# A windowed-attention and gated-MLP kernel on one core: the listed order of its steps between 18 and 75 microseconds replaced by another

## The chip, the cores and the metric

The kernel runs on one core of one Trainium2 chip. A core has a matrix engine (TensorE, PE in the profile), a vector engine (VectorE, DVE), a scalar engine (ScalarE, ACT), GpSimd (POOL), SyncE (SP), which here issues nearly all loads and stores, and 16 DMA engines that carry them out. Each engine runs its own instructions strictly in the order in which they were given to it; engines wait for one another by semaphores. The metric is the device time of one execution in microseconds (us); lower is better.

## What is computed

Eight batch entries ("blocks" here) go through a causal attention with a window of 64 positions, and the result through a gated MLP in which one half is normalised, mixed over the positions and multiplied with the other half. Cut to what matters:

```python
# attention: q, k, v are (8, 8 heads, 576 positions, 64)
scores = scale * np.matmul(q, k.transpose(0, 1, 3, 2))
mask = (rel >= 0) & (rel < 64)
attn = softmax(np.where(mask, scores, -1e9))
x = (attn @ v).transpose(0, 2, 1, 3).reshape(8, 576, 512)
# gated MLP
h = np.maximum(x @ w_in, 0.0)                  # w_in (512, 1024)
u, v = h[..., :512], h[..., 512:]
v_n = (v - mean(v)) / np.sqrt(var(v) + 1e-6)
v_s = np.einsum('ts,bsd->btd', w_spatial, v_n) + b_spatial[None, :, None]
out = (u * v_s) @ w_out                        # float32
```

## The kernel before

The kernel is one long list of 1,111 named steps. A step is one small piece of work: one load, one cast, or one group of matmuls into one accumulator bank. The text `ORDER` at the top of the file gives for each step its engine and, where it needs a buffer, the number of that buffer, and `as_listed` hands the steps out in that order. Per engine the order in the text is the order of execution; between engines the order is kept only where data or a buffer passes on. So `ORDER` decides three things: in which order an engine works, which engine does a cast or copy that several can do, and which earlier work a step must wait for because it takes over its buffer. The order was made by a planner ahead of time; no planner runs in the kernel.

A name has a letter for the kind of step, then the block, then the part. For one block b:

- `ldk`, `ldq`, `ldv`: loads of k, q (576 KB, for one half of the heads) and v (five pieces of up to 128 KB); SP issues them (lines 401 and 422). `ck`, `cq`, `cv`: casts to float16; `tk`, `tq`: transposes on VectorE (line 408); `sl`, `su`, `s4`: copies that make a second v, shifted by 64 positions (lines 293 to 301, the helper `cp`).
- `S`: scores of 64 small matmuls into a pair of banks (line 470); `E`: exponential on ScalarE (477); `M`: masking on VectorE (480); `Z`: row sums on TensorE (493); `N`, `n`: logarithm and exponential on ScalarE, which give the inverse (519, 521); `P`: attention times v on TensorE (504); `X`: the product with the inverse on VectorE (512). The last 64 positions have their own steps with `_r`.
- `V`: the half of x @ w_in that is normalised (653; the fifth one at 666 also carries the last output rows of the block before it); `Vr`: relu on ScalarE (633); `Vb`, `Va`: statistics on VectorE (635, 637); `L1`, `L2`: their inverse square root on ScalarE; `A`: the normalisation on VectorE (692). `U`, `Ur`: the other half and its relu (708, 721). `G`, `Ge`: the mixing over positions and the product (738, 752). `O`, `Oe`, `st`: output matmul, copy and store (763, 610).
- Once, early: `ldwin`, `cwin` for the eight pieces of w_in (`cwin1..` belong to V, `cwin0..` to U; the last two digits are the input rows), `ldwsp`, `cwsp`, `W`, `We` for w_spatial, which is transposed on TensorE, `ldwo`, `cwo` for w_out, and 25 `D` steps of two matmuls each on zeros (791), which keep TensorE busy at the start.

Four single banks (0 to 3) and two pairs (0:1) are shared by all matmul steps. A step that takes a bank waits until the step that had it before was read: a V step's bank is free when its `Vr` has run, a G step's when its `Ge` has. The number behind a step's engine in `ORDER` is that bank or buffer. TensorE does attention for block b+1 between the matmuls of block b's MLP.

VectorE, ScalarE and GpSimd can all do the early casts and copies (blocks 0 and 1 and the weights); for later blocks ScalarE and GpSimd alone, since `cost(...)` leaves VectorE out. On GpSimd a cast of 1,152 columns is three instructions.

## Time and profile before

| | us |
|---|---|
| median of 3 runs | 201.6 (201.12 to 201.91) |
| the profiled execution, device time | 201.67 |
| its span on the core | 200.0 |
| TensorE busy, at a granted clock of 1.00 throughout | 189.5 |
| ScalarE busy | 166.7 |
| VectorE busy | 160.9 |
| GpSimd busy | 78.0 |

The span runs from the first to the last instruction of the core; 1.67 us of the device time lie around it. The page cuts the span in 40 slices of 5 us and shows the busy share of each in tenths:

```profile
PE   7788899999999999999999999999999999999992
...
DVE  4699959999998999799699899979957795647430
```

From the sixth slice on TensorE is 90% or more busy in every slice but the last. The same rows show how full VectorE is from 30 to 75 us. Busy times are shares of the engine's time, not of its speed.

### The profile page before, as it was taken

Reading aid. Unit: us, or ns where it says so; the run is one execution under the profiler, and the core shown is the slowest. Engines: PE = TensorE matmul, PEld = TensorE weight load, DVE = VectorE, ACT = ScalarE, POOL = GpSimd, SP = SyncE. Lnnn points to the kernel's source line nnn. Section 1 sums busy time; section 2 is a strip of 40 time slices with the busy share of each in tenths; the row PEclk is TensorE's granted clock in tenths of the full one; section 3 lists DMA queues with packets and bytes.
Section 4 is the critical chain, followed back from the end, with each engine's and each line's share of the span. In section 5 each row is a group of like instructions: output and inputs, shape, how many; then the busy total and the mean of one; then the engine's idle time right before and its main releaser. Section 6 shows DMA issues by size and latency. Waiting matters only on the chain.

```text
span 200.0 us, 7013 instructions
## 1 busy us (share of the span) xinstructions
PE 189.5 (95%) x2927; PEld 97.8 (49%) x2927; DVE 160.9 (80%) x306; ACT 166.7 (83%) x307; POOL 78.0 (39%) x147
## 2 busy tenths in 40 slices
PE   7788899999999999999999999999999999999992
PEld 2333435645446445654455545554465455444450
DVE  4699959999998999799699899979957795647430
ACT  2598789887999899997998999999999999467431
POOL 5232574784995397252745999000000000000000
PEclk9999999999999999999999999999999999999999
DMA  6997999999899866898959996996723003200345
GB/s 224 378 284 175 362 374 209 303 374 377 168 258 281 278 182 195 260 277 210 333 123 259 245 293 224 244 285 226 187 109 118 3 7 131 108 0 0 133 143 201
DMA packets 50276, 42.69 MB, mean 214 GB/s; under 512 B 39362, under 2 KB 39490, under 8 KB 50243
## 3 DMA queue, kind: packets, MB, share of 16 engines
q1 hardware_dynamic: 50018, 41.91, 70.5%
q8 instruction: 23, 0.38, 0.8%
q10 hardware_dynamic: 224, 0.33, 0.5%
q14 instruction: 11, 0.08, 0.2%
HBM read 32.79 MB, written 9.44 MB: 211 GB/s over the span
## 4 chain that ended last, share of the span: by engine, by line
PE 72%; ACT 9%; SPq 6%; DMA 5%; DVE 3%; issue 1%; POOL 1%
PE bank L738 18%; PE bank L763 13%; PE bank L653 12%; PE bank L708 10%; SPq L422 4%; PE pair L470 3%; PE bank L504 3%; PE bank L493 3%; PE bank L666 3%; DMA wi<-in_moe_w_in_dram 3%; PE bank L744 3%; DMA nk<-in_k_dram 2%; ACT vs L633 2%; ACT ru L721 2%; PE bank L713 2%; ACT e L477 1%
## 5 line engine op out<-in xcount | busy, mean ns | idle before, releaser
L738 PE MATMUL bank<-wspT,vn 128*128 128x512 f16 (+1 forms) x160 | 37.5, 379 | 0.0
L477 ACT ACTIVATE e<-pair 128x1024 f16<-128x1024 f32 x32 | 31.8, 1027 | 2.7 <-PE pair L470 2.4
L752 DVE TENSOR_TENSOR g<-bank,ru 128x512 f16<-128x512 f32 (+1 forms) x40 | 24.8, 631 | 10.9 <-PE bank L738 5.9
L653 PE MATMUL bank<-win,x 128*128 128x512 f16 x128 | 30.8, 379 | 1.0 <-POOL win L301 0.8
L708 PE MATMUL bank<-x,win 128*128 128x512 f16 x128 | 31.6, 379 | 0.0
L763 PE MATMUL bank<-wout,g 128*128 128x512 f16 x128 | 31.3, 379 | 0.0
L635 DVE BATCH_NORM_STATS2 st<-vs 128x6 f32<-128x512 f16 (+1 forms) x40 | 25.9, 670 | 3.8 <-ACT vs L633 3.5
L721 ACT ACTIVATE ru<-bank 128x512 f32<-128x512 f32 (+1 forms) x40 | 21.4, 562 | 8.4 <-PE bank L708 4.6
L633 ACT ACTIVATE vs<-bank 128x512 f16<-128x512 f32 (+1 forms) x40 | 22.9, 596 | 3.2 <-PE bank L653 2.3
L610 ACT COPY ob<-bank 128x512 f32<-128x512 f32 (+1 forms) x39 | 22.6, 589 | 3.3 <-PE bank L763 3.1
L512 DVE TENSOR_TENSOR x<-bank,lz 128x512 f16<-128x512 f32 x32 | 21.2, 683 | 4.9 <-PE bank L504 2.2
L738 PEld LDWEIGHTS <-vn 128*128 128x128 f16 (+1 forms) x160 | 15.0, 97 | 17.7 <-issue 0.4
L480 DVE TENSOR_TENSOR e<-e,mask 128x1024 f16<-128x1024 f16 x32 | 22.4, 719 | 1.0 <-ACT e L477 1.0
L296 POOL CAST hq<-nq 128x384 f16<-128x384 f32 x33 | 17.2, 557 | 13.0 <-DMA nq<-in_q_dram 12.4
L408 DVE STREAM_TRANSPOSE qT<-hq 128x576 f32<-128x576 f32 x16 | 19.7, 1243 | 2.5 <-POOL hq L296 2.3
L296 POOL CAST hk<-nk 128x384 f16<-128x384 f32 x30 | 14.8, 526 | 17.4 <-DMA nk<-in_k_dram 17.2
L519 ACT ACTIVATE lz<-bank 128x512 f32<-128x512 f32 x32 | 18.6, 603 | 2.6 <-PE bank L493 2.5
L408 DVE STREAM_TRANSPOSE kT<-hk 128x576 f32<-128x576 f32 x16 | 20.0, 1247 | 0.7 <-ACT hk L293 0.4
L521 ACT ACTIVATE lz<-lz 128x512 f32<-128x512 f32 x32 | 19.6, 636 | 0.1
L653 PEld LDWEIGHTS <-x 128*128 128x128 f16 x128 | 11.9, 97 | 15.4 <-DVE x L583 1.1
L708 PEld LDWEIGHTS <-win 128*128 128x128 f16 x128 | 11.8, 98 | 14.4 <-issue 1.3
L763 PEld LDWEIGHTS <-g 128*128 128x128 f16 x128 | 11.8, 98 | 13.4 <-issue 0.5
(84 smaller groups left out, 297.2 us busy)
## 6 DMA issues: line engine op xcount, KB each, us to landing
nq<-in_q_dram SPq DMA_DIRECT2D x16, 576.0 KB, 6.0
nk<-in_k_dram SPq DMA_DIRECT2D x16, 576.0 KB, 6.1
nv<-in_v_dram SPq DMA_DIRECT2D x64, 128.0 KB, 5.6
out_dram<-ob SPq DMA_DIRECT2D x14, 512.0 KB, 4.3
wi<-in_moe_w_in_dram SPq DMA_DIRECT2D x8, 256.0 KB, 6.9
ws<-in_moe_w_spatial_dram SPq DMA_DIRECT2D x4, 288.0 KB, 6.4
...
```

The costliest lines, as they stand in the source:

```text
L296: nc.gpsimd.tensor_copy(o[:, n:n + 384], i[:, n:n + 384])
L408: d = add(f"t{name}{b}_{g}", ("DVE", 1.09), key, lambda e: nc.vector.transpose(qt.t[:, :].rearrange("p (i j) -> p j i", j=18), h.t[:, :].b ...
L477: ex = add(f"E{b}_{g}{u}", ("ACT", 0.91), key, lambda e, u=u: nc.scalar.activation(e2[u].t[:, :, :], sc[u].t[:, :, :], AF.Exp, bias=0.0, s ...
L610: lambda e: (nc.vector.tensor_copy if last else nc.scalar.copy)(view(), m.t[rows, 0:n]),
L633: rl = add(f"Vr{b}_{j}", ("ACT", 0.49), key, lambda e: nc.scalar.activation(vs.t[0:jn, :], m.t[0:jn, :], AF.Relu), deps=[pv], acq=[vs], us ...
L635: s1 = add(f"Vb{b}_{j}", ("DVE", 0.6), key + 0.02, lambda e: nc.vector.bn_stats(st6.t[0:jn, 0:6], vs.t[0:jn, :]), deps=[rl], acq=[st6], us ...
L653: nc.tensor.matmul(m.t[:, :], xr(b, r)[:, 128 * j:128 * j + 128], w_in_sb[r][:, 512:1024], start=(r == 0), stop=(r == 3))
L708: nc.tensor.matmul(m.t[:, :], w_in_sb[r][:, 128 * i:128 * i + 128], xr(b, r), start=(r == 0), stop=(r == 3))
L721: lambda e, m=m, ru=ru, n=n: nc.scalar.activation(ru.t[:, 0:n], m.t[:, 0:n], AF.Relu), deps=[pu], acq=[ru], uses=[m])))
L738: nc.tensor.matmul(m.t[:, :], w[0:kn, 128 * i:128 * i + 128], wspT[kk][0:kn, 0:512], start=(kk == 0), stop=(kk == 4))
L752: lambda e, m=m, g=g, ru=ru, n=n: nc.vector.tensor_tensor(g.t[:, 0:n], m.t[:, 0:n], ru.t[:, 0:n], ALU.mult),
L763: nc.tensor.matmul(m.t[:, :], G[r][0].t[:, 128 * j:128 * j + 128], w_out_sb[r][:, :], start=(r == 0), stop=(r == 3))
```

## The change

The text `ORDER` is replaced between 18 and 75 us. The list was chosen by a planner anew, judged on 24 scattered draws. The multiset of steps is the same, 1,111. Before 18 us each engine runs the same steps in the same order. Behind about 80 us the order within each engine is the same too: the last 167 of 287 TensorE steps, the last 165 VectorE steps, the last 191 ScalarE steps, the last 26 GpSimd steps and the last 69 of SP's agree. Buffer numbers differ from there on as well, because each buffer goes on from another place.

26 casts and copies change their engine:

| from, to | steps |
|---|---|
| GpSimd to VectorE | sl0_01, cwin110, cwin101, cwsp3, sl1_01, su1_01, su1_10 |
| ScalarE to VectorE | cwin100, We4 |
| VectorE to GpSimd | su0_10, cv0_11, sl0_11, cwsp4 |
| VectorE to ScalarE | We0 |
| GpSimd to ScalarE | s40_0, cq1_1, s41_1, su1_11, ck2_1, cwo00 |
| ScalarE to GpSimd | cwin000, cwin001, s41_0, sl1_10, sl1_11, cwo10, cwo01 |

TensorE's order from the first V step to block 1's first V step, before and after:

```
before  V0_1 V0_2 Z1_00 V0_0 V0_3 Z1_01 V0_4 S1_1 U0_2 U0_3 U0_4 U0_1 S1_r Z1_11 U0_0 W0 W2 W3 W4 W1
        Z1_r P1_01 P1_00 Z1_10 G0_4 G0_3 G0_0 G0_2 G0_1 P1_10 P1_11 S2_0 P1_r V1_2
after   V0_0 V0_3 V0_2 Z1_00 V0_4 V0_1 S1_1 U0_0 U0_3 U0_4 U0_1 U0_2 S1_r Z1_10 Z1_11 W1 W4 W0 W2 W3
        Z1_01 P1_00 P1_01 G0_4 Z1_r G0_2 G0_3 G0_0 P1_11 P1_10 G0_1 S2_0 P1_r V1_1
```

Among the loads the pieces of w_in come as 101, 110, 111, then 010, 000, 011, 001 behind k and q of block 1 (before: 110, 111, 101, 000, then k and q, then 001, 010, 011), w_spatial's and w_out's pieces change places, and `ldv5_10` moves from just before `ldv3_10` to just behind `ldv4_10`.

In the code one line changes: the A steps may also be given to GpSimd by a planner. No entry of the new list does so.

The diff, with the lists cut to about the first half of what differs:

```diff
@@ -16,134 +16,134 @@
 BIG = 65504.0
 
 ORDER = """
...
-sl0_00:DVE:1 Z0_r:PE:2 su0_00:DVE ldwin111:DQ Z0_11:PE:0 N0_r:ACT:3 D9:PE:3 n0_00:ACT cv0_01:DVE
-ldwin101:DQ D8:PE:1 su0_01:DVE sl0_01:POOL n0_10:ACT su0_10:DVE D13:PE:2 ldwin000:DQ:1 ldb:DQ:0
-n0_01:ACT tk1_0:DVE:5 s40_0:POOL ldk1_1:DQ:2 N0_11:ACT:4 P0_01:PE:3 ldq1_1:DQ:3 P0_00:PE:1 n0_11:ACT
-cv0_11:DVE ldwin001:DQ S1_0:PE:0:1 sl0_11:DVE X0_00:DVE:0 D20:PE:2 su0_11:POOL cwin110:POOL
-ldwin010:DQ:4 E1_00:ACT:1 s40_1:DVE D19:PE:0 ldwin011:DQ X0_01:DVE ldwsp3:DQ:5 E1_01:ACT:0
-cwin111:POOL P0_10:PE:1 P0_11:PE:2 X0_10:DVE:1 D18:PE:0 cwin100:ACT cwin101:POOL ldwsp2:DQ:7 D3:PE:3
-n0_r:ACT X0_11:DVE M1_00:DVE cwin000:ACT M1_01:DVE ldwsp1:DQ:6 P0_r:PE:0 cb:ACT V0_1:PE:3 X0_r:DVE:0
-V0_2:PE:2 Z1_00:PE:1 ck1_1:POOL:2 ldwsp4:DQ:0 Vr0_1:ACT:0 N1_00:ACT:5 Vb0_1:DVE:0 V0_0:PE:0
-Vr0_2:ACT:1 tk1_1:DVE:0 cq1_1:POOL:3 ldv1_00:DQ:2 V0_3:PE:3 Vr0_0:ACT:2 n1_00:ACT ldwsp0:DQ:2
-Z1_01:PE:1 tq1_1:DVE:1 V0_4:PE:2 cwin001:ACT cwin010:POOL ldv1_01:DQ N1_01:ACT:2 cwin011:POOL
-Vr0_3:ACT:3 ldv1_02:DQ Vb0_2:DVE:1 S1_1:PE:0:1 Vr0_4:ACT:4 Vb0_0:DVE:2 cwsp3:POOL ldv1_03:DQ
-U0_2:PE:0 E1_11:ACT:2 Vb0_3:DVE:3 cwsp2:POOL ldv1_04:DQ U0_3:PE:1 Va0_2:DVE Va0_3:DVE E1_10:ACT:3
-Va0_1:DVE Vb0_4:DVE:4 cwsp1:POOL ldk2_0:DQ:3 U0_4:PE:3 Va0_0:DVE Va0_4:DVE M1_11:DVE L10:ACT:0
-ldv1_10:DQ:3 U0_1:PE:2 Ur0_3:ACT:0 M1_10:DVE Ur0_2:ACT:1 ldv1_11:DQ S1_r:PE:1:0 cwsp4:DVE L20:ACT
-Z1_11:PE:1 Ur0_1:ACT:2 A0_4:DVE ldq2_0:DQ:1 U0_0:PE:0 cwsp0:DVE E1_r0:ACT:1 E1_r1:ACT ldv1_12:DQ
-A0_0:DVE:0 Ur0_4:ACT:3 A0_3:DVE:1 W0:PE:2 N1_11:ACT:1 ldv1_13:DQ cv1_00:DVE:2 W2:PE:3 M1_r:DVE
-Ur0_0:ACT:4 cv1_01:POOL W3:PE:1 We0:DVE ldv1_14:DQ sl1_00:ACT:2 We2:DVE ldk2_1:DQ:4 W4:PE:0
-s41_0:ACT su1_00:DVE We3:ACT sl1_01:POOL W1:PE:2 su1_01:POOL A0_2:DVE:2 We4:ACT Z1_r:PE:3 P1_01:PE:1
-A0_1:DVE:3 N1_r:ACT:0 We1:DVE ck2_0:POOL:0 ldwo10:DQ:5 P1_00:PE:0 Z1_10:PE:3 X1_00:DVE:2 G0_4:PE:2
-ldq2_1:DQ:7 N1_10:ACT:4 G0_3:PE:0 n1_01:ACT X1_01:DVE tk2_0:DVE:2 cv1_10:POOL:3 ldwo00:DQ:6
-n1_10:ACT sl1_10:ACT:3 G0_0:PE:3 su1_10:POOL cq2_0:ACT:1 ldwo11:DQ Ge0_3:DVE:0 G0_2:PE:1 ldwo01:DQ
-Ge0_4:DVE:1 tq2_0:DVE:3 cv1_11:POOL ldq3_0:DQ:0 G0_1:PE:0 ldv2_00:DQ:0 s41_1:POOL sl1_11:ACT
-su1_11:POOL n1_r:ACT Ge0_2:DVE:2 P1_10:PE:2 n1_11:ACT X1_10:DVE:3 ck2_1:POOL:2 P1_11:PE:1
-ldk3_0:DQ:2 S2_0:PE:1:0 X1_11:DVE cwo10:ACT ldv2_01:DQ P1_r:PE:2 Ge0_0:DVE:3 V1_2:PE:1 E2_00:ACT:0
-X1_r:DVE:1 Ge0_1:DVE:4 E2_01:ACT:1 V1_1:PE:3 cq2_1:POOL:3 ldv2_02:DQ tk2_1:DVE:0 V1_3:PE:2
-Vr1_2:ACT:5 ldv2_03:DQ cwo00:POOL Vr1_1:ACT:6 tq2_1:DVE:1 U1_2:PE:0 ldv2_10:DQ:1 Vr1_3:ACT:7
-cwo11:ACT ldv2_11:DQ V1_0:PE:1 M2_00:DVE Ur1_2:ACT:5 Vb1_2:DVE:5 cwo01:ACT S2_1:PE:1:0 Vr1_0:ACT:4
-M2_01:DVE Z2_00:PE:3 cq3_0:POOL:0 ldv2_04:DQ E2_10:ACT:3 V1_4:PE:2 Vb1_1:DVE:1 ldv2_12:DQ Va1_2:DVE
-Vb1_3:DVE:3 U1_1:PE:0 Vr1_4:ACT:2 M2_10:DVE Oe0_4:ACT:0 O0_0:PE:1 ck3_0:POOL:1 ldv2_13:DQ
-Vb1_4:DVE:0 E2_11:ACT:2 Vb1_0:DVE:2 ldq4_0:DQ:3 O0_2:PE:2 Oe0_0:ACT:0 Va1_3:DVE ldv2_14:DQ Va1_4:DVE
-Va1_1:DVE Ur1_1:ACT:0 Va1_0:DVE S2_r:PE:1:0 M2_11:DVE Z2_10:PE:1 cv2_00:POOL:1 ldv3_00:DQ:2
-L11:ACT:1 O0_1:PE:0 tq3_0:DVE:4 L21:ACT Oe0_2:ACT:1 ldq3_1:DQ:1 N2_10:ACT:3 U1_4:PE:2 ldk3_1:DQ:4
-A1_4:DVE E2_r0:ACT:0 U1_0:PE:1 N2_00:ACT:5 A1_0:DVE:4 ldv5_10:DQ:3 A1_2:DVE:5 Ur1_4:ACT:3 A1_1:DVE:6
...
+sl0_10:DVE:0 cv0_00:DVE:1 ldv0_13:DQ M0_r:DVE N0_01:ACT:1 sl0_00:DVE:1 ldv0_14:DQ Z0_r:PE:2
+su0_00:DVE N0_00:ACT:2 Z0_11:PE:0 cv0_01:DVE D9:PE:3 ldwin101:DQ su0_10:POOL D13:PE:1 ldb:DQ:7
+cwin100:DVE D8:PE:3 ldwin110:DQ:0 s40_0:ACT sl0_01:DVE n0_00:ACT ldwin111:DQ su0_01:DVE tk1_0:DVE:5
+cv0_11:POOL P0_00:PE:1 ldk1_1:DQ:1 N0_r:ACT:3 P0_01:PE:3 n0_01:ACT ldq1_1:DQ:2 su0_11:POOL
+ldwin010:DQ:3 n0_10:ACT s40_1:DVE S1_0:PE:0:1 sl0_11:POOL X0_00:DVE:0 ldwin000:DQ:4 N0_11:ACT:4
+ldwin011:DQ cwin101:DVE cb:ACT P0_10:PE:2 X0_01:DVE ldwin001:DQ P0_11:PE:1 n0_11:ACT D3:PE:0
+ldwsp2:DQ:5 cwin110:DVE E1_01:ACT:0 D20:PE:3 cwin111:POOL X0_10:DVE:1 ldwsp4:DQ:6 D18:PE:0 X0_11:DVE
+D19:PE:3 n0_r:ACT E1_00:ACT:1 M1_01:DVE P0_r:PE:2 V0_0:PE:0 ck1_1:POOL:2 ldv1_00:DQ:2 X0_r:DVE:0
+M1_00:DVE V0_3:PE:1 Vr0_0:ACT:0 Vb0_0:DVE:0 V0_2:PE:3 cq1_1:ACT:3 ldwsp1:DQ:7 tk1_1:DVE:0 Z1_00:PE:2
+cwin010:POOL ldwsp0:DQ:0 V0_4:PE:0 Vr0_3:ACT:1 Vr0_2:ACT:2 cwin000:POOL ldwsp3:DQ:1 tq1_1:DVE:1
+V0_1:PE:1 N1_00:ACT:5 cwin011:POOL ldv1_01:DQ Vr0_4:ACT:3 Vb0_2:DVE:1 n1_00:ACT S1_1:PE:1:0
+cwin001:POOL ldv1_02:DQ Vb0_3:DVE:2 Vr0_1:ACT:4 U0_0:PE:3 cwsp2:POOL ldv1_03:DQ E1_10:ACT:2
+Vb0_4:DVE:3 cwsp4:POOL Va0_0:DVE U0_3:PE:2 Vb0_1:DVE:4 E1_11:ACT:3 M1_10:DVE ldv1_04:DQ U0_4:PE:0
+Ur0_0:ACT:0 Va0_1:DVE cwsp1:POOL Va0_3:DVE U0_1:PE:1 Va0_4:DVE ldk2_0:DQ:2 Va0_2:DVE M1_11:DVE
+Ur0_4:ACT:1 ldv1_10:DQ:3 L10:ACT:0 L20:ACT U0_2:PE:3 Ur0_3:ACT:2 cwsp0:DVE A0_0:DVE:0 Ur0_1:ACT:3
+S1_r:PE:1:0 cwsp3:DVE Ur0_2:ACT:4 Z1_10:PE:0 A0_4:DVE Z1_11:PE:2 ldv1_11:DQ cv1_00:DVE:2 E1_r0:ACT:1
+W1:PE:1 N1_11:ACT:2 A0_1:DVE:1 ldq2_0:DQ:3 A0_3:DVE:2 W4:PE:3 cv1_01:POOL sl1_00:ACT:2 We1:DVE
+ldv1_12:DQ N1_10:ACT:1 W0:PE:2 su1_00:DVE s41_0:POOL We4:DVE W2:PE:1 E1_r1:ACT ldv1_13:DQ We0:ACT
+A0_2:DVE:3 W3:PE:0 su1_01:DVE sl1_01:DVE Z1_01:PE:3 ck2_0:POOL:0 We2:DVE We3:ACT P1_00:PE:2
+ldv1_14:DQ M1_r:DVE P1_01:PE:1 N1_01:ACT:0 X1_00:DVE:2 G0_4:PE:0 ldwo00:DQ:4 n1_01:ACT ldk2_1:DQ:5
+Z1_r:PE:3 Ge0_4:DVE:0 G0_2:PE:2 n1_11:ACT ldq2_1:DQ:6 cv1_10:POOL:3 tk2_0:DVE:2 ldwo10:DQ:7
+sl1_10:POOL:3 cq2_0:ACT:1 ldwo01:DQ G0_3:PE:0 X1_01:DVE ldwo11:DQ N1_r:ACT:4 Ge0_2:DVE:1 cv1_11:POOL
+ldq3_0:DQ:0 G0_0:PE:1 s41_1:ACT ldk3_0:DQ:1 su1_10:DVE su1_11:ACT sl1_11:POOL Ge0_3:DVE:2
+ldv2_00:DQ:0 n1_10:ACT tq2_0:DVE:3 P1_11:PE:3 cwo00:ACT P1_10:PE:2 G0_1:PE:0 n1_r:ACT X1_10:DVE:3
+ck2_1:ACT:2 ldv2_01:DQ X1_11:DVE S2_0:PE:1:0 Ge0_0:DVE:3 P1_r:PE:2 E2_00:ACT:1 V1_1:PE:3
+cq2_1:POOL:3 ldv2_02:DQ X1_r:DVE:1 tk2_1:DVE:0 E2_01:ACT:0 U1_2:PE:1 ldv2_03:DQ cwo10:POOL V1_3:PE:2
+Vr1_1:ACT:5 tq2_1:DVE:1 Ur1_2:ACT:5 cwo01:POOL V1_2:PE:3 Vr1_3:ACT:6 M2_00:DVE cwo11:ACT V1_0:PE:1
+M2_01:DVE Vr1_2:ACT:7 cq3_0:POOL:0 Vb1_3:DVE:5 Z2_00:PE:2 ldv2_10:DQ:1 Vr1_0:ACT:0 S2_1:PE:1:0
+Ge0_1:DVE:4 N2_00:ACT:3 V1_4:PE:3 Vb1_0:DVE:0 E2_10:ACT:3 ck3_0:POOL:1 Vb1_2:DVE:4 Z2_01:PE:1
+Vr1_4:ACT:3 O0_2:PE:0 Vb1_1:DVE:2 ldv2_11:DQ E2_11:ACT:2 Vb1_4:DVE:3 ldv2_12:DQ U1_1:PE:2 M2_10:DVE
+ldv2_13:DQ cv2_00:POOL:1 Oe0_2:ACT:0 Va1_4:DVE S2_r:PE:1:0 Oe0_4:ACT:0 Va1_0:DVE ldk3_1:DQ:2
+Va1_2:DVE Va1_3:DVE U1_0:PE:0 Va1_1:DVE L11:ACT:1 ldv2_04:DQ L21:ACT N2_01:ACT:5 A1_0:DVE:4
+ldv2_14:DQ O0_0:PE:3 A1_1:DVE:5 Ur1_1:ACT:1 A1_3:DVE:6 ldq3_1:DQ:3 Ur1_0:ACT:4 U1_4:PE:1 A1_4:DVE
+ldq4_1:DQ:5 A1_2:DVE:7 Oe0_0:ACT:1 U1_3:PE:2 ldv3_10:DQ:2 M2_11:DVE sl2_00:ACT:0 su2_00:POOL
+ldv3_11:DQ tq3_0:DVE:4 O0_1:PE:0 Ur1_3:ACT:2 ldv3_12:DQ Ur1_4:ACT:0 G1_1:PE:3 E2_r0:ACT:0
+cv2_10:POOL:0 tk3_0:DVE:5 ldv3_13:DQ E2_r1:ACT Oe0_1:ACT G1_0:PE:2 Ge1_1:DVE:5 sl2_10:POOL:1
+s42_1:ACT s42_0:ACT ldq4_0:DQ:6 n2_01:ACT Z2_11:PE:1 Ge1_0:DVE:6 Z2_10:PE:0 su2_10:POOL n2_00:ACT
+P2_00:PE:3 S3_0:PE:1:0 N2_11:ACT:0 X2_00:DVE:0 ldv3_00:DQ:3 P2_01:PE:2 N2_10:ACT:1 cq3_1:POOL:2
...
@@ -691,7 +691,7 @@
                 o = vn.t if vn is not None else vn4_t[b % NSB]
                 ENG[e].tensor_scalar(o[0:jn, :], VS[j].t[0:jn, :], mv_t[b % NSB][0:jn, j, 0:1],
                                      ln.t[0:jn, 5 + j:6 + j], ALU.subtract, ALU.mult)
-            AP.append(add(f"A{b}_{j}", ("DVE", 0.33), key + 0.2, emit_A,
+            AP.append(add(f"A{b}_{j}", [("DVE", 0.33), ("POOL", 0.6)], key + 0.2, emit_A,
                           deps=[l2] + (GDONE.get(b - NSB, []) if j == 4 else []),
                           acq=[vn] if vn else [], uses=[VS[j], ln]))
         LNDONE[b] = AP
```

## The prediction

> **What bounds the kernel now.** I read the page's busy table first, then busy time by stretch, then the chain of waits from 15 to 50 us, then the operations grouped by line and shape, then VectorE's, GpSimd's and the DMA queue's rows in order of time. Times are from the span's start.

> ```profile
> span 200.0 us, 7013 instructions
> PE 189.5 (95%) x2927; PEld 97.8 (49%) x2927; DVE 160.9 (80%) x306; ACT 166.7 (83%) x307; POOL 78.0 (39%) x147
> ...
> core 0: us, PE busy (x) PEld busy (x) DVE busy (x) ACT busy (x) POOL busy (x), PEclk, DMA share, GB/s
> 18.00:30.00 12.00, 10.41 (x172) 4.88 (x170) 9.63 (x16) 10.12 (x19) 7.92 (x14) 1.00 1.00 335
> 30.00:46.50 16.50, 15.78 (x339) 9.54 (x338) 15.85 (x35) 14.03 (x31) 10.22 (x19) 1.00 1.06 305
> 46.50:60.00 13.50, 13.42 (x171) 6.46 (x171) 13.50 (x27) 13.06 (x25) 11.68 (x19) 1.00 0.97 253
> 60.00:82.00 22.00, 22.00 (x362) 11.24 (x362) 19.98 (x36) 20.76 (x42) 14.15 (x27) 1.00 0.80 239
> ```

> The granted clock is 1.00 throughout. TensorE (PE) is out of work for 1.6 us before 30 us, 0.7 us from 30 to 46.5, 0.1 us from there to 60 and nowhere from 60 to 82. So a planner can win in the first two rows alone, and whatever TensorE is early or late when block 1's V steps start is carried through a full TensorE. But VectorE (DVE) is as full as TensorE in those rows: 15.85 of 16.5, then 13.50 of 13.50 us. It is the second bound, and the change gives it more.

> ```profile
> 17.96 6.00 DMA wi<-in_moe_w_in_dram
> ...
> 24.02 1.16 POOL win L301
> ...
> 25.22 1.67 PE bank L653 x7
> ...
> 39.22 0.45 DVE wspT L301
> ...
> 39.71 0.76 PE bank L744 x20
> ...
> 45.83 0.69 DVE x L512
> ...
> 46.56 2.75 PE bank L653 x12
> ```

> The chain of waits gives the two places. The first V step needs a weight (ldwin101) that lands at 23.96 and whose cast on GpSimd (POOL) takes until 25.18; from 39 to 46.5 VectorE's products and copies release TensorE (We1 before G0_4, X1_11 before V1_2).

> **The change, part by part.** TensorE's multiset of steps is the same, so its own work changes only by the order. A step of four 128x512 matmuls starts 0.86 us after the one before; beside a Z, P or fifth V step the spacing grows by 0.10 us. From D13 to P1_r I count 22 such changes of step kind, S steps included, against 21, and from there to P3_00 17 against 19: +0.1 and -0.2 us.

> ```profile
> L301 DVE CAST hv<-nv 128x512 f16<-128x512 f32 x5 | 2.1, 415 | 0.0
> L301 DVE CAST wnat<-ws 128x576 f16<-128x576 f32 x1 | 0.4, 443 | 0.0
> L301 POOL CAST win<-wi 128x512 f16<-128x512 f32 x5 | 3.7, 744 | 1.6 <-DMA wi<-in_moe_w_in_dram 1.6
> L293 ACT CAST hk<-nk 128x1152 f16<-128x1152 f32 x6 | 6.9, 1156 | 4.6 <-DMA nk<-in_k_dram 4.6
> ...
> 17.80 0.91 DVE L301 COPY hs<-hv 64x512 f16<-64x512 f16 x2
> 20.29 0.29 DVE L301 COPY hs<-hv 64x512 f16<-64x512 f16 x1
> 37.52 0.53 DVE L301 COPY hs<-hv 64x512 f16<-64x512 f16 x1
> ```

> *First V step.* ldwin101 goes from third to first of the three weight loads behind ldv0_14, and cwin100, cwin101, cwin110 go to VectorE. The trace's landings of the first, second and third weight there are 20.93, 21.80 and 23.96. VectorE's queue from cv0_01 (ends 17.77), by start spacings: three weight casts at 0.42 (the row of the same shape), sl0_01 and su0_01 at 0.29, tk1_0 1.10, s40_1 0.27, four X at 0.60 to 0.68: 1.26 + 0.58 + 1.10 + 0.27 + 2.48 = 5.69, so X0_11 ends at 23.5, or 24.4 if the three casts or copies under GpSimd work lose the 0.3 that the 17.80 row shows (0.91 for two copies of 0.29). It ended at 23.49 before. On TensorE P0_10 and P0_11 now wait for sl0_11 on GpSimd (three ops after ldv0_13's landing at 18.58: about 21.1), then the four warm-ups take 1.73 and P0_r some 0.4: V0_0 at 24.0. Before, the unbroken batch would have begun at 25.0 (25.22 less one matmul of 0.22). Gain 1.0 us; 0.5 if the third weight, now cwin111's, lands at 23.96 again, since only V0_0's fourth matmul needs it; 0 is the low end.

> *Casts onto ScalarE (ACT).* cq1_1 leaves GpSimd (1.41 us, three pieces) for ScalarE (1.15), behind Vr0_0. Its load landed at 27.56; with one weight less ahead of it (0.7 to 0.9 us between landings) about 26.7. ScalarE is there at 25.7, waits, and is done at 27.9; Vr0_3, Vr0_2, N1_00 and Vr0_4 are queued behind. V0_1 reuses V0_3's bank, so it waits for Vr0_3, 28.4, where TensorE arrives at 27.9: 0.5 us lost (0 to 1.3). ck2_1, s41_1, su1_11 and cwo00 also come to ScalarE, but cwin000, cwin001, cwo10, cwo01, sl1_10, sl1_11, We4 and others leave: about 5.0 us each way. Its 1.4 us of free time from 30 to 46.5 hides the exchange; without it ck2_1 would hold E2_00 back by its 1.15.

> *VectorE from X0_r to X1_11.* This sets V1. Before: 25.03 to 46.51, 21.48 us, of which idle 1.67, 0.26, 0.14, 0.29 and 0.30 stand in the rows: 18.8 of work. The change adds in this stretch cwsp3 and We4 (0.44 each), su1_01, sl1_01 and su1_10 (0.35 each, between 0.29 and 0.53), takes cwsp4 and We0 (0.44 each) away, and brings M1_00 (0.60) in from ahead of it: 20.5. X0_r ends at about 24.6, since M1_00 now follows it. The waits that I find along the new queue are Vb0_0 for Vr0_0 0.55, tk1_1 for ck1_1 0.4, and some 0.45 at M1_10, cwsp3 and Ge0_4: 1.4. So X1_11 ends at 24.6 + 20.5 + 1.4 = 46.5, and 46.8 with 0.3 for clashes with GpSimd, which I take. V1_1 starts 0.3 us later than V1_2 did: the front's gain is eaten. Bounds: 46.1 without any clash and with 0.4 less waiting; 48.8 if all five added small operations and three of the neighbours lose 0.25 each (0.53 against 0.29) and the waits grow by 0.3.

> The trace shows the clash as 0.53 and 0.91 us rows where a lone copy takes 0.29. [...]

> *Loads.* All moved loads but one stay within a few places in SP's queue. The weight loads take each other's places; ldwo00 goes ahead of ldk2_1 and ldq2_1 (cover: cwo00 is not needed before O0_2, some 9 us later); ldv3_02, ldv3_03 and ldv3_04 no longer stand behind st0_1, for which SP waited from 66.83 to 71.21; ldv5_10 goes back 24 us, to about 81, and is cast after 100. Cost nothing on the path; if ldwo00 pushed ldk2_1 back by one load, 0.9 us, ck2_1 and E2_00 would be late by as much.

> *After V1.* TensorE has 0.1 us to gain in waits and 0.2 in kind changes. VectorE does block 1's five A steps ahead of M2_11 and tq3_0 (0.60 and 1.10), where G1_1 used to start at 59.36 while the last A (A1_3, 59.30 to 59.77) ran. That covers the 0.3 of lateness. I take -0.3; -0.6 to +0.5.

> The POOL alternative added to the A steps is not used by the list: every A step still says DVE. It costs nothing.

> Sum: +0.3 - 0.3 = 0. The profiled execution took 201.67 (span 200.0 and 1.67 around it), the runs' median is 201.6. Forecast: 201.6, its own range 200.8 to 202.5.

> **Rivals.** *A, the front's gain stays.* If VectorE's queue keeps 0.9 us of the earlier Vb0_0 (its first statistics step could start at 25.75 instead of 26.69) because its waits close up, V1 starts 1.0 early and the later 0.3 stays: 201.6 - 1.3 = 200.3. For it: the first two rows have 2.3 us of idle TensorE. Against: 15.85 of 16.5.

> *B, VectorE overfull (slower).* Between 36 and 46 us GpSimd casts and copies almost without a break. Each of su1_01, sl1_01, We2, We4 and su1_10 then takes its row's clashed length; su1_01 also waits on VectorE for GpSimd's cv1_01 (its row: 1.20 us instead of 0.61), with sl1_01, We2, M1_r and X1_00 behind it. P1_00 and G0_4 need them. Price: 8 x 0.25 + 0.6 = 2.6 less the 0.8 of front gain left: 203.4. It decides once We2 ends past 39.7, where We1 ended before. For it: 13.50 of 13.50 next, so no recovery before 60. Against: the list has them in another order than GpSimd's, and 19.98 of 22 us after 60.

> *C, ScalarE held by loads.* If ldq1_1 lands at 27.56 as before, cq1_1 ends at 28.7, Vr0_3 at 29.2, and V0_1 waits 1.3 us; the chain to tq1_1 and S1_1 (30.37 before) moves along: 201.6 + 1.3 = 202.9. Against: fewer bytes ahead of it.

> **How the numbers follow.** 0.5%, 1.0 us, is about what a measurement of this kernel tells from none (its three runs spread 0.8 us). Forecast 0.38, A 0.25, B 0.25, C 0.12. Faster 0.25 is A, same 0.38 the forecast, slower 0.37 B and C. The range runs from A's time to a little past B's: 200.3 to 203.8; the tails beyond hold about 0.1 each.

> **What would show it.** Right: first full V0 step near 24.0 with no wait over 0.5; one wait of about 0.5 at V0_1 ended by a ScalarE vs; X1_11 ending at 46.5 to 47.1, VectorE without idle from 30 to 46; O1_0 starting within 0.5 of its 79.92 before. Wrong: V1_1 before 46.0 (A), We2 past 39.7 and V1_1 past 47.5 (B), cq1_1 ending past 28.5 (C), or a wait behind 82 us, where the order per engine is nearly the old one.

## The result, and the profile after

The changed kernel takes 203.05 us (median of 20 executions, 202.22 to 207.54) against 201.77 us of the kernel before beside it (20 executions, 200.54 to 204.90): a ratio of 1.0073, with a 95% interval of 1.0050 to 1.0095. It is slower by 0.7%. A ratio here and in the table below is not that of the two medians, and it leaves out executions more than 1.5% above the fastest of their kernel: one of this kernel, two of before, seven of the twelve of e11. The profiled execution took 204.26 us, 1.2 above the median; its span is 202.4.

The busy table, the slices and the busy time by stretch, in the stretches that were shown of before (columns: the stretch, its length, then each engine's busy time, the granted clock, the DMA share):

```profile
span 202.4 us, 7014 instructions
PE 190.4 (94%) x2927; PEld 98.9 (49%) x2927; DVE 162.8 (80%) x310; ACT 167.6 (83%) x305; POOL 77.8 (38%) x141
...
PE   7678898899998999999999999999999999999991
...
PEclk9999999979999999999999999999999999999999
...
18.00:30.00 12.00, 10.74 (x208) 5.54 (x207) 10.98 (x19) 10.00 (x18) 6.21 (x10) 1.00 0.96 301
30.00:46.50 16.50, 15.12 (x251) 8.87 (x233) 14.75 (x34) 14.66 (x29) 8.07 (x13) 0.90 1.11 310
46.50:60.00 13.50, 13.50 (x253) 6.83 (x248) 12.33 (x24) 11.51 (x21) 11.75 (x19) 1.00 0.98 260
60.00:82.00 22.00, 21.49 (x358) 11.40 (x357) 21.14 (x36) 20.62 (x41) 16.14 (x31) 1.00 0.90 264
```

Read it against before, stretch by stretch. Up to 30 us TensorE gained 0.33 us of work (10.74 against 10.41): the front is faster. From 30 to 46.5 it lost 0.66 (15.12 against 15.78), and a new number stands there: a clock of 0.90. From 60 to 82 it lost another 0.51 (21.49 against 22.00), where before it had no wait at all.

The waits of TensorE from 28 to 47 us, longest first (total, times, longest), and the chain of waits there (start, length, what):

```profile
PE bank L504 <- DVE hs L301: 0.7, 1, 0.7
PE bank L708 <- POOL win L301: 0.5, 1, 0.5
```

```profile
22.07 7.15 DMA wi<-in_moe_w_in_dram
...
29.24 6.63 DMA nv<-in_v_dram
...
35.90 0.43 DVE hv L301
36.32 0.20 DVE vn L692
...
37.37 0.60 DVE hs L301
...
38.00 0.45 DVE wspT L301
...
38.48 0.41 DVE vn L692
...
38.91 0.29 DVE hs L301
...
39.22 0.51 DVE hs L301
...
39.77 1.00 PE bank L504 x18
```

The first wait is P1_00's: it starts at 38.72, stops after eight matmuls and goes on at 39.77, when sl1_01 (39.22 to 39.71) has been copied. From 39.77 on TensorE has no idle time up to V1_1, so this wait, and not X1_11, decides when V1_1 starts. VectorE's chain ahead of it is work with no gap over 0.04 us: cv1_00, A steps, We1, su1_00, We4, A0_2, su1_01, sl1_01. The second wait is U0_0's, for cwin001, the last of the U weights to land, cast on GpSimd from 30.63 to 31.25.

The last reading is the clock. The same table cut at the places where the granted clock changes:

```profile
32.92:36.33 3.41, 3.41 (x66) 1.72 (x64) 2.90 (x9) 3.02 (x9) 1.28 (x2) 1.00 1.22 263
36.33:39.75 3.42, 2.57 (x31) 1.81 (x31) 3.30 (x9) 3.19 (x8) 1.71 (x4) 1.00 1.07 297
39.75:43.16 3.41, 3.40 (x51) 2.50 (x52) 2.36 (x5) 2.42 (x4) 2.08 (x5) 0.50 1.16 297
43.16:46.57 3.41, 3.41 (x46) 1.67 (x44) 3.35 (x6) 3.19 (x6) 1.12 (x2) 1.00 1.02 388
```

TensorE ran at half its clock for 3.41 us, right behind the stretch with P1_00's wait. V1_1 starts at 48.78 (V1_2 before: 46.56), so 2.2 us are lost by then, the half clock's share included; O1_0 starts at 82.48 (before 79.92), and the 2.2 to 2.6 us are carried to the end. The half clock explains why this execution lies above the median; it can't explain the median, since most executions of after have a mean clock of 0.995 or more (17 of the 20, median 202.91).

### The profile page after: what moved, and what is told of

It is laid out like the page before. It is cut to its first block, busy times and chain, and to the rows that moved or that the text cites. A ratio compares the mean times of both kernels' runs of the same rounds, so it can differ in the third digit from the quotient of the medians.

```text
span 202.4 us, 7014 instructions
## 1 busy us (share of the span) xinstructions
PE 190.4 (94%) x2927; PEld 98.9 (49%) x2927; DVE 162.8 (80%) x310; ACT 167.6 (83%) x305; POOL 77.8 (38%) x141
## 4 chain that ended last, share of the span: by engine, by line
PE 71%; DMA 8%; SPq 7%; ACT 7%; DVE 4%; issue 1%
PE bank L738 18%; PE bank L763 12%; PE bank L653 11%; PE bank L708 10%; SPq L422 5%; DMA nv<-in_v_dram 5%; PE bank L504 4%; PE pair L470 4%; DMA wi<-in_moe_w_in_dram 4%; PE bank L666 3%; PE bank L493 3%; PE bank L744 3%; PE bank L713 1%; ACT ob L610 1%; SPq L401 1%; DVE vn L692 1%
## 5 line engine op out<-in xcount | busy, mean ns | idle before, releaser
L738 PE MATMUL bank<-wspT,vn 128*128 128x512 f16 (+1 forms) x160 | 38.1, 383 | 0.0
L653 PE MATMUL bank<-win,x 128*128 128x512 f16 x128 | 30.4, 379 | 0.2 <-ACT vs L633 0.2
L721 ACT ACTIVATE ru<-bank 128x512 f32<-128x512 f32 (+1 forms) x40 | 21.1, 558 | 8.7 <-PE bank L708 4.6
L512 DVE TENSOR_TENSOR x<-bank,lz 128x512 f16<-128x512 f32 x32 | 21.1, 683 | 4.8 <-PE bank L504 2.2
L480 DVE TENSOR_TENSOR e<-e,mask 128x1024 f16<-128x1024 f16 x32 | 23.2, 744 | 0.7 <-ACT e L477 0.7
L296 POOL CAST hq<-nq 128x384 f16<-128x384 f32 x30 | 16.1, 573 | 17.4 <-DMA nq<-in_q_dram 16.0
L296 POOL CAST hk<-nk 128x384 f16<-128x384 f32 x27 | 15.3, 602 | 13.5 <-DMA nk<-in_k_dram 11.7
L692 DVE TENSOR_SCALAR vn<-vs,mv,ln 128x512 f16<-128x512 f16 (+1 forms) x40 | 16.0, 451 | 4.3 <-ACT ln L682 4.0
L653 PEld LDWEIGHTS <-x 128*128 128x128 f16 x128 | 12.0, 98 | 14.7 <-issue 1.0
```

Source lines behind the costliest of these rows:

```text
L296: nc.gpsimd.tensor_copy(o[:, n:n + 384], i[:, n:n + 384])
L480: mins.append(add(f"M{b}_{g}{u}", ("DVE", 0.65), key, lambda e, u=u: nc.vector.tensor_tensor(e2[u].t[:, :, :], e2[u].t[:, :, :], mask[:, : ...
L653: nc.tensor.matmul(m.t[:, :], xr(b, r)[:, 128 * j:128 * j + 128], w_in_sb[r][:, 512:1024], start=(r == 0), stop=(r == 3))
L738: nc.tensor.matmul(m.t[:, :], w[0:kn, 128 * i:128 * i + 128], wspT[kk][0:kn, 0:512], start=(kk == 0), stop=(kk == 4))
```

## The experiments

Each ratio is against before on the same chip, with its 95% interval. "V" is the start of block 1's first V step, "O1_0" that step's start, both in the kernel's one profile and as a difference to before (46.56 and 79.92). A "fall" is an execution with a mean clock of 0.992 or less; one stretch of 3.41 us at 0.50 takes 0.0085 off the mean of a 201 us span. A profile is one execution: of the 136 executions of before with a mean clock of 0.995 or more, four fifths lie between 200.9 and 203.3 us, so an offset of half a microsecond in V or O1_0 is not firm. The last column, the least stream, is explained under the clock below.

```
kernel                              ratio   interval          falls    V      O1_0   least stream
after, 20 executions                1.0073  1.0050..1.0095    3 of 20  +2.22  +2.56  0.34 f
after again (e0)                    1.0057  1.0025..1.0090    1 of 12  +0.58  +0.83  0.56
e1 U weights in order of use        1.0049  1.0013..1.0086    5 of 12  +2.36  +2.69  0.34 f
e2 four operations to GpSimd        1.0038  1.0002..1.0073    3 of 12  +0.55  +0.19  0.56
e3 before, those four on VectorE    1.0050  1.0015..1.0084    3 of 12  +0.92  +0.93  0.51
e4 after to S1_1, then before       1.0200  1.0141..1.0259    4 of 6   +4.85  +5.27  0.35 f
e5 before to S1_1, then after       1.0165  1.0114..1.0215    6 of 6   +2.90  +2.60  0.18 f
e6 e1 and e2 together               1.0100  1.0052..1.0148    2 of 6   +2.72  +2.70  0.34 f
e7 e4, U weights in order of use    1.0130  1.0078..1.0183    5 of 6   +4.46  +4.69  0.20 f
e8 after, wait filled               1.0067  1.0030..1.0103    0 of 12  +0.11  +0.65  0.55
e9 before, ldwin101 first           1.0015  0.9984..1.0045    0 of 12  -0.31  -0.31  0.43
e10 e11 with U0_2 moved             1.0030  0.9996..1.0063    2 of 12  +3.92  +3.56  0.20 f
e11 e6, M1_r earlier                1.0067  1.0019..1.0116    7 of 12  +2.54  +2.88  0.33 f
e12 after to V1_1, then before      1.0065  1.0026..1.0104    0 of 12  +0.86  +1.00  0.35
e13 before to V1_1, then after      1.0031  1.0006..1.0056    0 of 12  +0.05  +0.85  0.62
e14 e1, wait filled                 1.0067  1.0030..1.0105    0 of 12  +0.68  +0.93  0.44
e15 e2, wait filled                 1.0033  0.9998..1.0069    0 of 12  +0.79  +1.13  0.58
e16 e13, M2_11 earlier              0.9980  0.9950..1.0011    0 of 12  +0.59  +1.27  0.57
e17 all of it mended, filled        1.0032  1.0006..1.0058    0 of 12  +0.78  +0.59  0.64
before, 139 executions beside them  1                         3 of 139 0      0      0.48
f: the clock fell right behind that window in this profile
```

### Is it the clock, the U weights or VectorE?

e0 is after, unchanged. The diffs from here on name only the words that differ.

> The changed kernel as it is, for a second profile. The first profile of it (span 202.4) has a stretch of 3.4 us from 39.7 in which the granted clock is 0.50; its other executions have a median of 203.05. Theory Q (the queues: V0's and U0's weights and an overfull VectorE hold TensorE back between 30 and 47 us): without that dip the span is about 201.2, TensorE waits 0.7 us in U0_0 and 0.9 us in P1_00 again, and V1_1 starts at 47.5 to 48.0 (before: V1_2 at 46.56). Theory K (the clock dips, and that alone makes it slower): without a dip the span is 200.0 to 200.4. Theory D (the DMA engines deliver later by chance): v's third and fourth piece of block 1 land within 0.3 us of 35.35 and 35.92, and the waits are gone.

This profile has no fall, and V is 0.58 late all the same; eleven executions without a fall have a median of 203.38 against 202.28. The clock alone doesn't make the loss, so theory K is out; theory D is out too, since the waits stayed and v's fourth piece (ldv1_03) landed at 36.88. Theory Q's span fits (201.1), its V1_1 (47.5 to 48.0) is missed: it starts at 47.14. TensorE's waits from 28 to 84 us in this execution:

```profile
PE bank L708 <- POOL win L301: 0.7, 1, 0.7
PE bank L504 <- DVE hs L301: 0.5, 1, 0.5
PE bank L653 <- ACT vs L633: 0.5, 1, 0.5
PE bank L504 <- DVE g L752: 0.4, 1, 0.4
```

As in the first profile, TensorE has no idle time between P1_01 (39.71) and V1_1. The last line is a wait behind V, P2_00's for Ge1_1; before has none there.

e1 loads and casts the U weights in the order in which U0_0 uses them.

```diff
-ldwin010 ldwin000 ldwin011 ldwin001   cwin010 cwin000 cwin011 cwin001
+ldwin000 ldwin001 ldwin010 ldwin011   cwin000 cwin001 cwin010 cwin011
```

> The changed kernel, with the four U pieces of w_in loaded and cast in the order in which U0_0's matmuls use them (000, 001, 010, 011 instead of 010, 000, 011, 001). U0_0 then waits for its fourth weight alone, and its wait falls from 0.7 to 0.2 us. Theory Q with both waits adding up: 0.4 to 0.5 us faster than the changed kernel. Theory Q with VectorE as the one bound: U0 and W are earlier, but the wait in P1_00 grows by as much, and the time stays within 0.2 us of the changed kernel's.

U0_0's wait is gone and W1 starts at 35.00 instead of 35.93, but P1_00 waits 0.93 us as in after. What the U weights cost is swallowed there, as the second case said.

e2 and e3 move the four operations that the change added to VectorE, in after back to GpSimd and in before onto VectorE.

```diff
-cwsp3:DVE su1_01:DVE sl1_01:DVE su1_10:DVE
+cwsp3:POOL su1_01:POOL sl1_01:POOL su1_10:POOL
```

> The changed kernel with four small operations taken from VectorE and given to GpSimd again: cwsp3, su1_01, sl1_01, su1_10 (about 1.6 us of VectorE's queue between 35 and 45). Theory Q with VectorE as the bound: X1_11 ends 0.8 to 1.4 us earlier than in the changed kernel, and the whole is 0.8 to 1.4 us faster, near the time of the kernel before. Theory K or D: within 0.3 us of the changed kernel.

> The other way round: the kernel before, with the same four operations moved from GpSimd to VectorE (cwsp3, sl1_01, su1_01 ahead of We1, su1_10 ahead of tq2_0; all else as it was). Theory Q with VectorE as the bound: We1 ends about 1.0 us later, G0_4 starts at 40.7, and the whole is 0.8 to 1.4 us slower than before, all of the change's loss. If GpSimd's casts get quicker because less clashes, 0.5. Theory K or D: no slower than 0.3.

e3 is the clearer one: four small operations on VectorE, 1.8 us in all and nothing else, make before slower by 0.5% and V late by 0.92 us, carried unchanged to O1_0. In e3's profile, from 28 to 47 us:

```profile
PE bank L504 <- DVE hs L301: 0.9, 2, 0.6
```

The wait is for the copies themselves, which VectorE now makes ahead of We1. So e3 doesn't part VectorE's added work from the place of the copies in its queue; no run has the same four at another place.

e2 keeps V 0.55 late, since P1_00 now waits as long for GpSimd's copies of the same data. The 0.8 to 1.4 us foretold didn't come: its ratio can't be told from that of after.

### Cutting the list in two at S1_1

e4, e5 and e7 take one list up to S1_1 (about 30 us) and the other list for all that is left. e6 is e1 and e2 together.

> After's list up to S1_1 (about 29 us), then before's list for every step that is left, with before's engines; buffers numbered anew. The four operations go back to GpSimd with it. Theory V (VectorE's added work from 30 to 46 us makes the loss, the front does not): P1_01 and G0_4 start no later than before's 37.9 and 39.71, block 1's first V step at 46.0 to 46.7 and the ratio to before is 0.996 to 1.001. Theory F (the loss comes from the front: the wait of the first U step for cwin001, later v loads): V step at 47.0 or later, ratio 1.003 to 1.007. If the front's gain can come through at all, the V step is at 45.8 to 46.2 and the ratio below 0.997.

> The first kernel of this call with the U weights loaded in the order 000, 001, 010, 011 and cast 000, 010, 011 on GpSimd, 001 on ScalarE. Theory V: the first U step 0.3 to 0.7 us earlier; block 1's V step the same within 0.3 us, as VectorE sets it; ratio within 0.002 of the first. Theory F: V step 0.3 to 0.7 earlier, ratio lower by 0.002 to 0.004.

Both miss, and they don't test what they were made for. After's front loads w_spatial's pieces in the order 2, 4, 1, 0, 3, before's rest casts piece 3 first, so that GpSimd stood still for it, with W0 and all that follows behind (GpSimd in e4, in order of time; idle time and its cause in brackets):

```profile
30.25 0.61 POOL L301 CAST win<-wi 128x512 f16<-128x512 f32 x1 [0.97 <-DMA wi<-in_moe_w_in_dram]
35.73 3.09 POOL L301 CAST wnat<-ws 128x576 f16<-128x576 f32 x3 [4.87 <-DMA ws<-in_moe_w_spatial_dram]
```

> Before's list up to S1_1, then after's list for every step that is left. Theory V: V1_1 starts at 47.0 to 47.7, as in the undisturbed profile of after (47.14), ratio 1.003 to 1.007, though the front is before's own. Theory F: V1_1 by 46.7, ratio within 0.998 to 1.002.

> After with the U weights in the order 000, 001, 010, 011 and the four operations on GpSimd (the edits of the two earlier runs together). Theory V: alone the first was swallowed at P1_00 and the second left a wait of 0.7 there; together V1_1 at 46.3 to 46.9 and the ratio 0.998 to 1.002. If GpSimd is the new bound in front of P1_00, V1_1 stays at 47.0 or later and the ratio at 1.002 to 1.006.

e5 fits neither case and is slower than the whole of after: the middle of the new list on the old front waits 1.2 us at P1_00, and all six executions have a fall. e6 took longer than either case. G0_4 starts at 39.22, half a microsecond ahead of before, but then Z1_r waits 0.9 us for M1_r. VectorE and GpSimd in e6:

```profile
38.43 2.42 DVE L553 TENSOR_TENSOR er<-er,maskr 128x512 f16<-128x512 f16 x1
```

```profile
37.38 1.28 POOL L301 COPY hs<-hv 64x512 f16<-64x512 f16 x2
38.62 1.40 POOL L296 CAST hk<-nk 128x384 f16<-128x384 f32 x3
39.97 0.61 POOL L301 CAST hv<-nv 128x512 f16<-128x512 f32 x1
40.64 0.47 POOL L301 COPY hs<-hv 64x256 f16<-64x256 f16 x1
```

The masking takes 0.41 us in before and in after. Here it ends at 40.85, 0.28 us behind the end of a row of GpSimd instructions from 37.38 to 40.57 with no gap over 0.06 us; after 0.06 us more the next one starts.

### What makes the clock fall

The falls come with the list: 6 of 6 executions in e5, 3 of 139 in before. In every profile the clock changes at multiples of 3.413 us from its first rise (after: 34.13 us, ten windows, up to the fall, and 3.41 for the fall itself). So I cut each trace into those windows and summed what TensorE streamed in each: for every matmul its columns, times the active columns of 128, times 0.42 ns (0.86 us for four of 512), divided by 3.41 us. The table's last column is the least of these from 28 to 47 us, up to a first fall. The eight profiles with a fall have 0.18 to 0.35 in the window ahead of it; the twelve without have 0.35 to 0.64. Busy time doesn't part them: after was busy for 2.57 of 3.42 us ahead of its fall, e3 for 66% of a window without one. The thin stretch is W's short matmuls, Z and P steps; P1_00's wait stands in it.

Counted more finely, these profiles have no exception. From the clock's first rise to the end, with the active rows of 128 as a second factor, and a matmul on the border of two windows split between them, the twenty profiles have 1,150 windows: the 33 that are followed by half clock (ten of them before 60 us, the others at the end of the kernel) have 0.339 or less, the 1,117 that are followed by full clock have 0.343 or more. W's transposes have to be counted in: without them two windows of some 0.09 (in e6 and e12) have no fall behind them.

e8 tests this by filling the wait with work that computes nothing: two more of the D steps on zeros.

```diff
-NWARM = 25
+NWARM = 27
-We3:ACT P1_00:PE:2
+We3:ACT D25:PE:2 D26:PE:2 P1_00:PE:2
```

> After with two more D steps (two 128x512 matmuls on zeros each, 0.86 us in all) on TensorE right ahead of P1_00, where it waits 0.7 to 0.9 us; nothing else. Theory G (the clock falls to 0.50 for 3.41 us after a 3.41 us window in which TensorE streams less than some 0.35 of what it could; the wait at P1_00 beside the small W and Z steps makes such windows): the windows from 30 to 46 us hold 0.45 or more, no execution has a mean clock under 0.995 (after itself: about one in three), V1_1 stays late at 47.0 to 47.6, since VectorE is untouched; ratio to before 1.003 to 1.006. Rival R (the falls have another cause, such as the chip or the hour): again a third of the executions between 0.983 and 0.993.

No window from 28 to 47 us is below 0.55 in its profile, and no execution of twelve has a fall. Together with e14, e15 and e17, which have the same filling, it is none of 48; the lists without it (after twice, e1, e2, e6) had 14 of 62, and e12 below, whose front is after's without the filling, none of 12 at a least stream of 0.35. The expectation of one in three for after was too high: it has 4 of 32. And the time didn't move (203.31, without a fall in any): the median's loss isn't the falls. They are a second loss on top, some 0.9 to 3.1 us in an execution that has one (medians with and without: e2 203.71 and 202.85, e1 204.20 and 202.61, e11 206.12 and 203.37, e10 205.64 and 202.53). V1_1 missed its mark, 46.67 instead of 47.0 or later, in a profile that is of the fastest of the twelve executions (201.88), and the ratio lies just above the 1.003 to 1.006 foretold.

### The front alone, and two attempts to beat before

e9 makes only the change's first step, in before.

```diff
-ldwin110 ldwin111 ldwin101   cwin110 cwin111 cwin101
+ldwin101 ldwin110 ldwin111   cwin101 cwin110 cwin111
```

> Before with ldwin101 first of the three weight loads and cwin101 first of GpSimd's three weight casts; nothing else. It is the change's step at the first V step alone. Rival A of the prediction (the front's gain can stay): first full V step at 24.0 to 24.4 and block 1's first V step at 45.6 to 46.2, ratio 0.995 to 0.998. Theory V (VectorE from 25 to 46.5 sets it whatever the front does): first V step early, block 1's at 46.3 to 46.7, ratio 0.999 to 1.002.

In its profile the first full V step, V0_1, takes 1.19 us instead of 2.04, since it no longer waits inside for the last weight. S1_1 starts 0.51 earlier and V at 46.25, 0.31 earlier, between the two cases, and the ratio shows no gain. A part of what the front wins is lost on the way to 46 us; that VectorE takes the rest too isn't shown.

e11 is e6 with M1_r moved ahead of A0_2 on VectorE; e10 also moves U0_2 from before S1_r to behind W0. Both also put E1_r1, which M1_r needs, behind We0 on ScalarE.

> The same without moving U0_2: both parts undone and M1_r ahead of A0_2. Theory L (a VectorE operation is held for as long as GpSimd works without a break): M1_r takes 0.4 to 0.8 us, Z1_r loses its wait of 0.9, and the window from 38 us rises from 0.34 to above 0.45; block 1's first V step at 46.2 to 46.8 and the ratio 0.998 to 1.002, with fewer falls of the clock than the two in six of the kernel without the move. If M1_r's length was chance, falls and ratio stay (1.006 to 1.012).

> The kernel in which both parts are undone, with M1_r moved ahead of A0_2 on VectorE (it took 2.42 us there behind four GpSimd casts in a row, otherwise 0.41) and U0_2 moved from before S1_r to behind W0, so that a full U step stands among the small ones. Theory G and V: windows from 30 to 46 us at 0.42 or more, no execution under 0.995, block 1's first V step at 46.0 to 46.6, ratio 0.996 to 1.000. If W1 waits for a w_spatial cast where U0_2 stood, 0.5 to 0.9 us of it come back: 1.000 to 1.004.

In e11 M1_r takes 0.58 us, but it has 7 falls in 12, not fewer, and its median over all twelve is 204.53 against 201.88. In e10 M1_r met GpSimd's row from 37.61 on, was held for 2.72 us again, and the window around it has 0.20. Neither beats before.

### Ahead of V or behind it?

e12 and e13 cut at V1_1 instead, and e14 and e15 repeat e1 and e2 with the wait filled.

> After's list up to V1_1 (block 1's first V step, about 47 us), before's list behind it, with before's engines. Theory V (the loss is made ahead of V1_1): ratio 1.004 to 1.008, as after, and falls of the clock in about one of eight executions. Theory T (the order behind V1_1 makes the loss of the undisturbed executions): 1.000 to 1.003.

> Before's list up to V1_1, after's behind it. Theory V: ratio 0.998 to 1.002 and no fall of the clock. Theory T: 1.003 to 1.007 without falls; P2_00 at 62.7 to 63.2 and O1_0 at 80.4 to 80.8 in the profile though V1_2 starts at 46.3 to 46.8.

> After with the U weights in the order 000, 001, 010, 011 and the two D steps ahead of P1_00. If the wait of the U weights is a part of the loss that comes through when the clock holds: no falls, ratio 1.000 to 1.004 (the executions of the unfilled kernel without a fall had a median of 202.6 against 202.3). If VectorE swallows it: 1.005 to 1.008, like the filled kernel without this edit (1.0067).

> After with cwsp3, su1_01, sl1_01 and su1_10 on GpSimd and the two D steps ahead of P1_00. Theory V: no falls, V1_1 at 46.4 to 47.0, ratio 1.001 to 1.004 (the unfilled kernel's executions without a fall: 202.85 against 202.28, 1.003). If these four don't matter: 1.005 to 1.008.

The part ahead of V alone makes as much as the whole (1.0065, no fall among twelve), and the part behind it makes a smaller loss of its own (1.0031). Whether the two add up in after can't be told within these intervals. e14 again shows no gain from the U weights (1.0067, as e8). e15 points to VectorE's four operations as some part of the loss ahead of V (1.0033 against 1.0067; the intervals overlap, and the medians of all executions give 1.0048 against 1.0071); its profile doesn't show it, with V1_1 at 47.35 instead of 46.4 to 47.0.

For the part behind V, TensorE's waits from 46.5 to 82 us in e13, and VectorE there:

```profile
PE bank L504 <- DVE g L752: 0.6, 1, 0.6
```

```profile
56.78 2.92 DVE L692 TENSOR_SCALAR vn<-vs,mv,ln 128x512 f16<-128x512 f16 x5 [0.92 <-ACT ln L682]
59.63 0.67 DVE L480 TENSOR_TENSOR e<-e,mask 128x1024 f16<-128x1024 f16 x1
60.23 1.24 DVE L408 STREAM_TRANSPOSE qT<-hq 128x576 f32<-128x576 f32 x1
61.33 1.23 DVE L408 STREAM_TRANSPOSE kT<-hk 128x576 f32<-128x576 f32 x1
62.41 1.26 DVE L752 TENSOR_TENSOR g<-bank,ru 128x512 f16<-128x512 f32 x2
```

VectorE is idle for 0.92 us, since the A steps need ScalarE's L21, and only then does the five A steps, M2_11, tq3_0 and tk3_0; Ge1_1 starts at 62.41 (before: 60.78), and P2_00, which takes over its bank, waits. Before does M2_11 and tq3_0 where VectorE is idle here.

The idle time isn't the whole of it. e2 has the same list behind V, and VectorE stands idle there as long, but no wait of TensorE follows: Ge1_1 starts 14.30 us behind V (before: 14.22, e13: 15.80). What differs is the five A steps. VectorE in e2, and GpSimd in e2 and in e13:

```profile
56.83 1.88 DVE L692 TENSOR_SCALAR vn<-vs,mv,ln 128x512 f16<-128x512 f16 x5 [0.91 <-ACT ln L682]
```

```profile
58.30 1.49 POOL L299 CAST hv<-nv 128x512 f16<-128x512 f32 x1 [1.03 <-DMA nv<-in_v_dram]
```

```profile
57.90 2.88 POOL L299 COPY hs<-hv 64x512 f16<-64x512 f16 x4
```

In e2 GpSimd waits for a piece of v from 57.27 to 58.30, and the A steps take 0.40 us each but for the first. In e13 GpSimd works beside all of them, and they take 0.48 to 0.75. All eleven profiles with the new list behind a late V go with this: from V to O1_0 they need 33.6 to 33.9 us where the five A steps take 2.7 to 3.1 (after, e0, e1, e8, e11, e14, e15), 33.0 to 33.3 where they take 1.7 to 2.6 (e2, e5, e6, e10); before needs 33.36.

e16 moves M2_11 back, in e13:

```diff
-L21:ACT N2_01:ACT:5 A1_0:DVE:4
+L21:ACT N2_01:ACT:5 M2_11:DVE A1_0:DVE:4
```

> e13 with one step moved: M2_11 on VectorE from behind block 1's A steps to ahead of them, where VectorE stood idle for 0.9 us. If the wait of P2_00 for Ge1_1 is the loss behind V1: Ge1_1 0.5 to 0.7 us earlier, P2_00's wait of 0.6 gone, O1_0 at 80.0 to 80.4 and the ratio 0.999 to 1.002. If not: O1_0 at 80.6 or later, ratio 1.002 to 1.005 as in e13.

The ratio falls from 1.0031 to 0.9980 (0.9950 to 1.0011), as the first case said. The profile is less clear: it is of the slowest of e16's twelve executions (202.66), where V is 0.59 late for reasons ahead of the edit, and P2_00's wait is 0.3 instead of 0.6, not gone; its O1_0 (81.19) missed. Ge1_1 comes 15.69 us behind V, only 0.1 less than in e13, since the A steps took 3.42 us here. So the ratio supports this wait as the part behind V, and the one profile doesn't. e16 is the best version found, and it can't be told from before.

> After with the U weights' order, the four operations on GpSimd, the two D steps ahead of P1_00 and M2_11 ahead of A1_0. If these places are the whole loss: no falls of the clock, V1_1 at 46.2 to 46.9, O1_0 at 79.6 to 80.3, ratio 0.998 to 1.002. If M1_r is held behind ck2_0 again (over 2 us), or another place loses as much: 1.003 to 1.007.

e17 has no fall and no wait of TensorE over 0.3 us from 28 to 84 us, and M1_r isn't held (0.56), yet its V1_1 (47.34) and O1_0 (80.51) are late and the ratio is 1.0032. Its two D steps, 0.86 us, no longer stand in a wait, and 0.86 of 202 us is 0.4%. That would explain it; a version without them wasn't run.

## Why the prediction was wrong

The forecast was no change, 201.6 us; it is 203.05, inside the range of 200.3 to 203.8, which it owes to rival B and not to the sum. Two terms of the sum failed, the 0.3 ahead of V and the -0.3 behind it. (The table of the change lists 27 steps that change their engine, not 26; nothing rests on the count.) The steps one by one:

**Right: the front.** V0_0 at 24.25 (24.0 foretold, for before's unbroken 25.0). cq1_1 from 26.75 to 27.90, as foretold; V0_1 waits for Vr0_3 and starts at 28.45 (28.4). S1_1 starts between 28.49 and 30.05 in the fourteen profiles with after's front, and between 30.02 and 30.66 in the five with before's. That the gain doesn't reach the end holds too: e9's ratio has none. That VectorE is what eats it was argued, and e9 doesn't show it.

**Wrong in size, and in where the wait stands: "VectorE from X0_r to X1_11. This sets V1", +0.3.** The sum of VectorE's work was good. In e0, the profile without a fall: X0_r ends at 25.07 (24.6), 20.3 us of work (20.5), 1.6 of waits (1.4), X1_11 ends at 46.99 (46.8). The clashes weren't it: su1_01 took 0.29 us and sl1_01 0.49 in after. But X1_11 doesn't release V1_1 in e0. TensorE comes to V1_1 at 47.14 without an idle moment since P1_01, where before waited 0.36 at G0_4 and 0.19 for X1_11. What the sum left out are TensorE's waits further up, at U0_0 and above all at P1_00, which needs VectorE's sl1_01 at 39.34, some seven microseconds ahead of the end of X1_11. Rival B named that dependence, the sum did not price it. The size: e12 has the new list up to V1_1 alone and no fall, its V is 0.86 late in the profile and its median 1.2 us above before's (203.25 against 202.03; the ratio's interval is 1.0026 to 1.0104), so the term is some 1.2 us instead of 0.3.

**Wrong: "After V1. ... I take -0.3".** The prediction's own table left 0.1 us of TensorE's waits to win there, and said that a late start is carried through a full TensorE. The step read block 1's A steps ahead of M2_11 and tq3_0 as cover for a late V all the same. It didn't ask whether the A steps' input is there (VectorE stood 0.92 us idle in e13), what they cost beside GpSimd's copies (2.92 us for five in e13, 1.88 in e2), nor who waits for Ge1_1 behind them: P2_00 does, for its bank. On an early V it is worth +0.4 us (e13: 202.45 against 202.03) instead of -0.3; its profile has 0.8 from V to O1_0. On a late V it is +0.25 in e0 and +0.34 in after; only where the A steps were not slowed did the -0.3 come (e2 and e10, -0.36). Without that -0.3 the sum had no zero to come to.

**Wrong, though free: "Cost nothing on the path" for the loads.** cwin001 became the last of the U weights, and U0_0's second matmul, which needs it, starts 0.91 (after) and 1.09 us (e0) behind the first, where 0.23 is usual; ldv1_01 lands at 35.87 instead of 34.90. No gain is seen without the first (e1, e14). What the second costs wasn't tried.

**Missed: the clock.** "The granted clock is 1.00 throughout" was read off before and taken along. Before's thinnest window has 0.48; the new order's waits bring it down to 0.34, and 4 of 32 executions fall. It isn't the median's loss.

**The rivals.** B gave the right sign and nearly the time (203.4), and in the profiled execution its marks are met (We2 ends at 40.07, V1_1 starts at 48.78). But its mechanism isn't what happened: the operations kept their length, su1_01 didn't wait for cv1_01 (done at 37.83), and V1_1 past 47.5 needed the fall. In e0 We2 ends at 39.65 and V1_1 starts at 47.14, short of both marks of B, and the kernel is slower all the same; O1_0 at 80.75 is outside the forecast's mark (within 0.5 of 79.92). A and C didn't happen: see e9, and cq1_1 at 27.90.

**What stays open:** half or more of the loss ahead of V, which is left with VectorE's four operations back on GpSimd (e15), isn't given to one cause; the later v loads and GpSimd's load are candidates, only argued. No run takes P1_00's wait away without putting D steps or GpSimd's copies in its place. How often the A steps meet GpSimd's copies isn't known either, since each kernel has one profile.
